# Twenty-nine half tiles masked on GpSimd in two passes, and the written order made anew

## The chip, the cores and the metric

The kernel runs on one core of a Trainium2 chip. The metric is the device time of one execution, in microseconds (us). A core has five engines with a queue each: TensorE (PE, matrix products, with its weight loads shown as PEld), VectorE (DVE), ScalarE (ACT), GpSimd (POOL) and SyncE (SP, which here only issues DMAs). GpSimd reads and writes SBUF, the on-chip memory; the products land in PSUM, from where VectorE and ScalarE take them.

## What is computed

Attention with a threshold, for 8 batches of 8 heads, 576 positions and 64 features, followed by a feed-forward layer whose hidden value is the largest of three products:

```python
scale = 1.0 / np.sqrt(q.shape[-1])
scores = scale * np.matmul(q, k.transpose(0, 1, 3, 2))
thresh = np.max(scores, axis=-1, keepdims=True) - tau            # tau = 0.02
scores = np.where(scores >= thresh, scores, -1000000000.0)
scores = scores - np.max(scores, axis=-1, keepdims=True)
attn = np.exp(scores)
attn = attn / (np.sum(attn, axis=-1, keepdims=True) + 1e-09)
out = np.matmul(attn, v)
# heads side by side: x is 4608 x 512
h = np.maximum(np.maximum(x @ w1, x @ w2), x @ w3)               # 512 -> 768
return h @ w_out                                                  # 768 -> 512
```

## The kernel before, in words

**Tiling.** A quad is four heads of one batch; there are 16 quads, two to a batch. A quad has nine chunks, and a chunk has two half tiles of 128 rows by 576 scores. That makes 144 chunks and 288 half tiles. The letters in brackets below are those of the order string.

**One half tile.** `scores` [S] makes 576 scores for each of 128 rows in PSUM. `maximum` [m] copies them to an SBUF tile `z` on VectorE with the sign turned and takes the row maximum on the way (`nm`). What follows depends on the half tile's digit in the string `MASKED`:

- digit 0: VectorE makes the threshold `th` [s]; ScalarE passes over `z` with Prelu [e], which leaves scores above the threshold nearly flat and keeps the others far off; ScalarE passes again with Exp and sums the row [n].
- digit 1: ScalarE passes once with Exp [e]; VectorE masks by comparing with exp(-tau), multiplies, and sums the row [k].
- digits 2 and 3: as 0 and 1, but the first ScalarE pass reads the scores from PSUM.

When both halves of a chunk have their sums, VectorE takes the reciprocals `rs` [r]; GpSimd multiplies each half by its reciprocal into the bf16 tile `P` [p, once a half]; SyncE issues a transposing DMA from `P` to `ptq` [t].

**The rest of the work.** [T] turns q and k on TensorE, [a] and [c] take them out of PSUM (a: ScalarE, c: VectorE or ScalarE), [q] makes the copy `qs` of q with its halves swapped (GpSimd, now and then VectorE). [O] is attention times v for a quad's two head pairs, [w] and [x] take it out to `xt`. [F] and [B] are the two parts of a piece of the feed-forward layer, for the hidden rows (`ph`) or for the output (`po`); [h] and [v] make the running maximum of the three products (h a copy on ScalarE, v a maximum on VectorE, into `hm` and at last `hT`); [u], [f], [j] copy the output, [o], [i], [d] store it. [l] loads q, k and v, [g] loads the weights to `stage` and [z] casts them on GpSimd; [y] casts v on GpSimd.

**What sets the order.** Nothing is scheduled when the kernel is built. `_Ordered` chains every engine's instructions in the order in which Python emits them, and Python emits them by reading the string `ORDER` letter by letter in `issue`. A digit behind S, T, O, F or N names one of four double banks of PSUM. So each engine's queue is its letters of `ORDER`, first to last, and an instruction that waits holds everything behind it on its engine. A later batch's scores and an earlier batch's feed-forward pieces are interleaved in this string. The last batch is split (`SPLIT`), so that its feed-forward layer comes in two parts.

**Buffers.** `z` has 9 buffers, and from the 73rd half tile on two more are taken from the pool `stage` (`half_of_z`), which is why the profile shows some half tiles under the name `stage`. `P` has 6 buffers, `hm` 3.

Of the kernel before, what the change touches and what calls it, by code (L numbers as in the profile page):

```python
# [21 lines left out]
FLAT = 2.0 ** -100  # L22

MASKED = """
220202110002002100110000100020020312000112012010100000000010100000001100
001000111010000101100000000000110001100000011110110200100000100010000000
110001101110100100010000001001100100000100101111102300000100100000001000
001000110100100001000000000100100001011110100011011100002100001000001013
"""


# [2 lines left out]
ZBUFS = 9  # L34
MORE_Z = 72
PBUFS = 6

SPLIT = {7: ((0, 1), (2, 3, 4))}
# [3 lines left out]
ytS1erkpT2agmnT3pclesqS2aqetS0meqlrnspmS1eqsT2nmpS3tnrcS0zlemS2eprmS3npmtS0npsgS1sermpS2emyS3eptmT0eplmS1ayl  # L42
meS0kynS2tssT3snkynkercperlT3pmnpmntqremS0lasprgeT3pmeS2psstnplnS0mzecesqrmS3etqkeS2gpnmS1npsmtnS0prmleS3pmS
2npsmnS0yrsmetperS2epmO1eqtnkplemnzswT2teS3rplS1empnmS3tpnssrS1klepS0mapermtS2epmT1S3nmqtnkO2qemncpS3txrskT1
# [12 lines left out]
S1lceBqmeptrskS0pulS3muS1epmS2teF0rmplnskpeS1mtO3eklekO2esrmpesBknpwxS1kutS2urmopS3nF0myeS1mBetpsmF2hlS3rkep
BlmnF0S1prnsvT3tepBmF2apsssvS1eBtqmeS0qrS3hmtS1epsmF2lnpF0mleF3koBnBrvpeBstyvS1phsS2nmF3emS0nrS1tpmBnprS2smn
F0pveF1pBsremT3ptevBpS2chF0tnmF3ekBT1nvS2aBsmlnF0qvS1eS2rtrespmS3eBmqF1hmpT2nBcpS3ekpT2O0sasvterlmpO2ekqntwS
3xklpS1eF2ssmnF0yrBnmyS3evBptemS1plhS2ssmT3eyF0rcpeF1mBpntT3vnByS2ravpS0nmtpS3nsmS1eF2srmpektepS3slmnS0Bmeqn  # L60
mT1ktuS3urS0lcpeO2rlmpelmpeO3klpelweF1kqnsxS0rkepS2tmS3eBymemepS0kuF3quT2smeBtrF1kphoS0aBmnpS3tsN2rnvplnmpS1
erkpF0tjsF3mnBpsseBvS2ihrS1pmelS0mqeF3S2mnytBpmnoS1rF0eprsvF2ntpmBeBvqF1htskpS3esS0rmetS2pnmF3pBnmF0pesvT2te
BcF1nsBrvpntBskphT2F3erS0vlapBmnF1qvS2etpBmT0hS3rscpnF2lmS1qesS0sempBemS3yF1nvtS0nmBnT2ssrmpO3etspveF0wnS1rk
BpaS3tmhS2elqsF1mlS0qnmS3ermpBF2espsmS0npvBeS3tmeS1rvpO0ntmnsmS2yxS3empF0eskyerT1mpeS2cBtnypsmelkS3ulS2muS1e
smT0O3nsrplnpO2awetmeF3rkpxseT0S1ycntS2meF0poBrnsmpnkpF1ukBurS2shBqemF3oepvS0lS2nsmqF1emBptBnvF0hrrS2speS3mp
F1emBpntT2vepF3BssaktS0nvlBemS2hS1rsmptF0nS3mpeBmtnT2F1svnF3cetBBsrnvpS2hsrqS0meS1pmeT3F2sprmaS0npBmeF3ptsvn
S1qS0mnBtqmeS2yF1prevS0epssBmnS3qmS2htpmF0nlF1keBsmBertvO3pnvepF0serwpT2nBcpF3hktS1eBsrsmpnT0S2vtpaS1remqT3S
0nmyF2qectT1BpasmS3epvS1nS0mqnF2rmpemtpT3eS1keqS0smBercntpS1mupS3emF0ukessS1rmtpnBmopkS2uskS1eO3rukekO0yxeO3
# [36 lines left out]
def kernel(  # L105
# [273 lines left out]
    def exponents(c, r):  # L379
        z = c["z", r]  # L380
        src, sign = (c[r], -1.0) if direct(c, r) else (z, 1.0)
        if masked(c["g"], c["idx"], r):
            scalar.activation(out=z, in_=src, func=AF.Exp, bias=c["nm", r], scale=-sign)
        else:
            th = c["nm", r] if direct(c, r) else c["th", r]
            scalar.activation(out=z, in_=src, func=AF.Prelu, bias=th, scale=sign, alpha=FLAT)

    def numerators(c, r):
        z, acc = c["z", r], c["sm"][:, r:r + 1]
# [89 lines left out]
    def ffn(b, part):  # L479
# [219 lines left out]
    def flow(what, fn):  # L699
        while True:  # L700
# [7 lines left out]
    line = {k: [] for k in "menkrptahvuxwcqsjf"}  # L708
# [10 lines left out]
    def issue(what, where):  # L719
# [27 lines left out]
        elif what == "m":  # L747
            c, r = line["m"].pop(0)
            maximum(c, r)
            line["e"].append((c, r))  # L750
            if not masked(c["g"], c["idx"], r) and not direct(c, r):
                line["s"].append((c, r))
        elif what == "s":
            threshold(*line["s"].pop(0))
        elif what == "e":
            c, r = line["e"].pop(0)
            exponents(c, r)
            line["k" if masked(c["g"], c["idx"], r) else "n"].append((c, r))
        elif what in "nk":
            c, r = line[what].pop(0)  # L760
            if "sm" not in c:
                c["sm"] = small.tile([128, 2], F32, name="sm")
            else:
                c["summed"] = True
            numerators(c, r)
        elif what == "r":
            c = made[line["r"].append(0) or len(line["r"]) - 1]
# [62 lines left out]
```

## Time and profile before

| what | value |
|---|---|
| runs | 442.97 us median of 3 (442.29 to 443.37) |
| profiled execution, first to last instruction | 440.2 us |
| instructions on TensorE (products), VectorE, ScalarE, GpSimd | 5188, 1248, 834, 420 |
| TensorE clock granted, mean | 0.988 of full |
| DMA | 88.50 MB in 213959 packets, 201 GB/s |
| transposing DMAs `ptq<-P` | 144, median 4.5 us from issue to landing |

The profile belongs to one execution; its span is the time from its first to its last instruction. What lies around the span (start and end of the launch) is not shown in it. The page gives each engine's busy time; the groups of instructions give count, busy time and the mean duration of one; the chain of waits follows the last instruction back to what released it, step by step. Every instruction of the program stands under L93, since a helper there records all of them, so they are told apart by the names of the tiles that they write and read, `out<-in`.

### The profile page before, as it was taken

The numbers are of one execution on the slowest core, as the hardware profiler recorded it, in microseconds if no ns is written. First come the engines' busy times: TensorE is split into PE (matmuls) and PEld (weight loads), VectorE is DVE, ScalarE is ACT, GpSimd is POOL, SyncE is SP. The second block draws the span as 40 slices with busy tenths as digits, with TensorE's granted clock in tenths as the row PEclk, the third lists the DMA queues.
The fourth block names the chain that finished last, engine by engine and source line by source line (L and its number), as shares of the span: only waits on it lengthen the run. The fifth ranks groups of instructions, "written<-read, shape, count | busy, mean of one in ns | idle before, by whom it ended". The sixth has DMA issues, their size and how long they took to land.

```text
span 440.2 us, 14283 instructions
## 1 busy us (share of the span) xinstructions
PE 418.9 (95%) x5188; PEld 313.6 (71%) x5190; DVE 393.9 (89%) x1248; ACT 403.6 (92%) x834; POOL 317.0 (72%) x420
## 2 busy tenths in 40 slices
PE   7696789999999999999999999999999999999996
PEld 6353446787788776787678777887688777786873
DVE  4888899999999999999999999999889999998542
ACT  4999999999999999999999999999999998989521
POOL 1988999998787778867786778886585776554400
PEclk9987999999999999999999999999999999999999
DMA  6999999999999999999999999999698778583812
GB/s 190 276 239 214 270 215 260 263 252 252 220 277 224 237 165 242 291 160 232 189 242 238 202 182 273 192 199 208 135 237 153 147 109 185 102 169 72 192 50 85
DMA packets 213959, 88.50 MB, mean 201 GB/s; under 512 B 189184, under 2 KB 202240, under 8 KB 213888
## 3 DMA queue, kind: packets, MB, share of 16 engines
q1 hardware_dynamic: 213360, 86.96, 95.4%
q8 instruction: 41, 0.67, 0.6%
q10 hardware_dynamic: 528, 0.62, 0.5%
q14 instruction: 30, 0.25, 0.2%
HBM read 35.65 MB, written 9.44 MB: 102 GB/s over the span
## 4 chain that ended last, share of the span: by engine, by line
PE 78%; DVE 5%; POOL 5%; issue 4%; ACT 3%; DMA 2%; SPq 1%; DVEq 0%; POOLq 0%; ACTq 0%
PE ph L93 31%; PE sc L93 26%; PE po L93 10%; PE o L93 8%; POOL P L93 4%; PE tp L93 3%; ACT z L93 3%; DVE z L93 3%; DMA qm<-in_q_dram 2%; SPq L93 1%; DVE kt L93 1%; POOL w L93 1%; DVE stage L93 0%; DVE hm L93 0%; POOL qs L93 0%
## 5 line engine op out<-in xcount | busy, mean ns | idle before, releaser
L93 POOL TENSOR_SCALAR P<-z,rs 128x576 bf16<-128x576 f32 x250 | 202.0, 819 | 59.1 <-DVE rs L93 30.4
L93 DVE TENSOR_SCALAR_CACHE_REDUCE z<-sc 128x576 f32<-128x576 f32 x250 | 183.2, 749 | 12.2 <-PE sc L93 8.1
L93 PE MATMUL sc<-kt,qs 64*128 64x256 f32 (+2 forms) x640 | 179.8, 417 | 5.5 <-DVE z L93 3.9
L93 PE MATMUL sc<-kt,qt 64*128 64x320 f32 (+2 forms) x640 | 180.9, 429 | 3.1 <-DVE z L93 1.2
L93 PE MATMUL ph<-xt,w 64*128 64x288 bf16 (+2 forms) x2160 | 172.0, 283 | 0.2 <-DVE hm L93 0.2
L93 PEld LDWEIGHTS <-w 64*128 64x128 bf16 (+1 forms) x2160 | 128.0, 94 | 31.6 <-issue 4.0
L93 ACT ACTIVATE z<-z,th 128x576 f32<-128x576 f32 x161 | 120.5, 767 | 2.2 <-DVE th L93 1.9
L93 ACT ACTIVATE z<-z 128x576 f32<-128x576 f32 x175 | 117.6, 674 | 0.2
L93 PEld LDWEIGHTS sc<-kt,qs 64*128 64x128 f32 (+1 forms) x640 | 92.4, 179 | 22.5 <-DVE z L93 8.6
L93 PEld LDWEIGHTS sc<-kt,qt 64*128 64x128 f32 (+1 forms) x640 | 92.0, 179 | 14.7 <-DVE z L93 3.5
L93 DVE SCALAR_TENSOR_TENSOR z<-z 128x576 f32<-128x576 f32 x75 | 61.7, 827 | 1.4 <-ACT z L93 1.1
L93 POOL COPY qs<-qt 64x640 f32<-64x640 f32 (+3 forms) x66 | 45.9, 695 | 19.5 <-ACT qt L93 16.1
L93 ACT ACTIVATE z<-z,nm 128x576 f32<-128x576 f32 x72 | 53.9, 767 | 0.0
L93 PE MATMUL po<-wo,hT 64*128 64x512 bf16 (+3 forms) x454 | 53.3, 354 | 0.3
L93 DVE TENSOR_TENSOR hm<-ph,hm 128x576 bf16<-128x576 f32 (+2 forms) x54 | 37.0, 685 | 9.8 <-PE ph L93 9.6
L93 ACT ACTIVATE hm<-ph 128x576 bf16<-128x576 f32 (+2 forms) x54 | 31.9, 590 | 14.3 <-PE ph L93 13.8
L93 PEld LDWEIGHTS <-hT 64*128 64x128 bf16 (+2 forms) x456 | 28.4, 95 | 18.5 <-issue 2.6
L93 DVE TENSOR_TENSOR hT<-ph,hm 128x576 bf16<-128x576 f32 (+2 forms) x54 | 36.9, 683 | 2.8 <-PE ph L93 1.0
L93 PE MATMUL o<-ptq,vb 128*64 128x512 bf16 (+2 forms) x544 | 38.7, 282 | 0.2 <-DVE z L93 0.2
L93 POOL TENSOR_SCALAR P<-stage,rs 128x576 bf16<-128x576 f32 x38 | 29.5, 783 | 11.7 <-DVE rs L93 8.4
L93 ACT ACTIVATION_READ_ACCUMULATOR z<-z 128x1 f32 x175 | 33.6, 192 | 0.0
L93 PEld LDWEIGHTS <-vb 128*64 128x64 bf16 x544 | 22.4, 111 | 14.0 <-issue 5.6
(44 smaller groups left out, 412.2 us busy)
## 6 DMA issues: line engine op xcount, KB each, us to landing
vm<-in_v_dram SPq DMA_DIRECT2D x32, 256.0 KB, 4.6
qm<-in_q_dram SPq DMA_DIRECT2D x15, 512.0 KB, 4.7
km<-in_k_dram SPq DMA_DIRECT2D x15, 512.0 KB, 5.4
out_dram<-ob SPq DMA_DIRECT2D x14, 512.0 KB, 4.5
stage<-in_moe_w_dram SPq DMA_DIRECT2D x9, 512.0 KB, 5.6
ptq<-P SPq DMA_TRANSPOSE x144, 4.5
vr<-in_v_dram SPq DMA_DIRECT2D x16, 128.0 KB, 3.8
stage<-in_moe_w_out_dram SPq DMA_DIRECT2D x3, 512.0 KB, 5.5
```

The lines of the kernel that those rows point to most:

```text
L93: ins = fn(*a, **kw)
```

## The change

Four things change together.

First, the string `MASKED` is another one, and it has a new digit, 4, on 29 of the 288 half tiles. A half tile with a 4 gets its maximum [m] and threshold [s] on VectorE as a 0 does. Then GpSimd makes two passes: `marked` [b] adds the threshold to `z`, multiplies by 2^100 and writes the result as int8 into the high bytes of a bf16 tile `far`, which so holds a very large number where the score is under the threshold and a zero elsewhere; `moved` [C] adds `far` to `z`. ScalarE then makes one pass with Exp that also sums the row [G]. The digits' counts are:

| digit | before | after |
|---|---|---|
| 0 | 187 | 174 |
| 1 | 84 | 69 |
| 2 | 14 | 10 |
| 3 | 3 | 6 |
| 4 | 0 | 29 |

Second, `ORDER` is written anew from the first letter to the last, with the letters b, C and G in it.

Third, `hm` has two buffers in place of three, and `far` is one new tile of 128x576 bf16, set to zero by VectorE at the start.

Fourth, the tile of row sums is made by whichever sum comes first (`summed`); this moves no work.

```diff
 MASKED = """
-220202110002002100110000100020020312000112012010100000000010100000001100
...
+241202210002302100100101300030022112000110010010010001000000100100001001
...
+FARS = 1
+FAR = 2.0 ** 100
...
 ORDER = """
-lllllllllT0laqqlcT1aS2lcqqgmS0S3lemS1lmnT2lmeS3lsaS0mnqlqemT3lyerclcapsnS1lS2eqmlS3qemznmS2perS1mnpsmnpT3ske
...
+llllllllllT1lacT2qqlaS1lqqcmgS3S2lemS0lnsS3mlbT1lmeClcelmayS0lGsT1lS3mqalceqlrS1mqelqmnS0lzS2eklpS1egmnprmnp
...
+    def on_pool(c, r):
+        return by_mask[2 * number[c["g"], c["idx"]] + r] == "4"
...
     def exponents(c, r):
         z = c["z", r]
         src, sign = (c[r], -1.0) if direct(c, r) else (z, 1.0)
+        if on_pool(c, r):
+            scalar.activation(out=z, in_=z, func=AF.Exp, bias=c["nm", r], scale=-1.0, accum_out=summed(c)[:, r:r + 1])
+            return
...
+    far = [one.tile([128, S], BF16, name=f"far{x}") for x in range(FARS)]
+    for t in far:
+        vector.memset(t, 0.0)
+    fars = iter(range(1 << 20))
+
+    def marked(c, r):
+
+        c["far", r] = t = far[next(fars) % FARS]
+        pool.tensor_scalar(out=t.bitcast(mybir.dt.int8).rearrange("p (n x) -> p n x", x=2)[:, :, 1],
+                           in0=c["z", r], scalar1=c["th", r], scalar2=FAR, op0=OP.add, op1=OP.mult)
+
+    def moved(c, r):
+        pool.tensor_tensor(out=c["z", r], in0=c["z", r], in1=c["far", r], op=OP.add)
...
-                    st["hm", f] = hp_.tile([128, nr, n], BF16, name="hm", bufs=3)
+                    st["hm", f] = hp_.tile([128, nr, n], BF16, name="hm", bufs=2)
...
         elif what == "s":
-            threshold(*line["s"].pop(0))
+            c, r = line["s"].pop(0)
+            threshold(c, r)
+            if on_pool(c, r):
+                line["b"].append((c, r))
+        elif what == "G":
+            exponents(*line["G"].pop(0))
+        elif what == "b":
+            c, r = line["b"].pop(0)
+            marked(c, r)
+            line["C"].append((c, r))
+        elif what == "C":
+            c, r = line["C"].pop(0)
+            moved(c, r)
+            line["G"].append((c, r))
```

More of the change, by code (lines that the diff above doesn't have):

```diff
@@ L36 @@
 PBUFS = 6
[L38 removed]
+FARS = 1
+FAR = 2.0 ** 100
+SPLIT = {7: ((0, 1), (2, 3, 4),)}
 ORDER = """
[L41 to L44 removed]
@@ new lines @@
+S2elqsmS0lnpskteprmepmnS3pmnS1qsermtpekS3epS2srtmeykeT1T0lnpmtaspknS0qsrS3emtpempncS0tpemnzsrS3smleT2S1ptmep
+rkeptncS0empS2nrS3mqtnS1mpeS0mplerklT3petmnT2psmS1ntrsS0kepsamyerS3cpS1epmtS2nmpO0emqtnmS3znrsO1lsweplmeygT0
+kyT3elS2cgxrsalmpS1eS0lkyS3ntpsmS2eprkO1epmnpmnS0qserO3mnqwepS2smS1xpktnF3ysremBpT0ermS2qthsspknF3pmatBS1epr
+vS0eztmF2eS3mpS1nlsmBpegF0svznlBkleF2S3grhmpBtnmF0peS1sssvqnBrmT3pnS2cF1eptrvBepS3mhpT0emT2zS1nsctS3nqmF2arg
+smBpelS0vpnS1mF3nzmBeS2grsesvpF1tS0esmqBnkpS3eF2mhyBmeF1rtvpF0nkBpeBstsvnS3zS2remS1hpgmeF0lpsmS3ezBsekO2nqgm
@@ new lines @@
+tnrvS1pnS3wyeF0prmT2npBmeS1psrvaO3zesmekpT0gS1xtcS2epS3mnF0qtsmF1nqrBsmeBpkhF2pteT3vBaS0zveS1mezS3mntS2qS0sr
+nmyF1epmlnlrpsskS3tnpS2meBpmtebrmF0uspulskelT2pS3cleS1CrlmnBtesmpS3ekpS2lnmO1ouqsrstmupO3ewyGkS0xprT1nF2myS3
+nypBamtS0hqF1srnmS3peBsmpS2etF0rspvnF3mqnBlsBplervS1lphF2smetpS0S3esbmF1ntBCkeF0BnmpBestvF3nsrS2vphtBrmnyS0e
+vtS2pGsmS3peF1mlS0pesrslmF2nylBympnBlvT3phlF0srcnS1tsT2eBmS3avS1eqmS2epF0tmnT3qBsmnpF1veS2tscBebF0mhoF3ekBtn
+rS1vpS2nmCBnF0srrmF1epBveT2ptkBhpF3asvBnptrS2veS0pmGS1ptT3snmF2pesrmpteS0scpnO1smqtersnpS3wS0lebmBlCmlelT1su
@@ new lines @@
+S0pluS3maO2nmGkT1ytxS0rscS3emS2pnS1mnyO0prmeqtmeO3psrewyekpS2lF1elmqnlskS0ptnBrxmpeokqS0luS3utmpF2nS1rmpeS0s
+rsBmebF3mhptT1BsakCF2esvS0eS1pmBeN3pmtnyskGoF0jprvlS1nS3primnF2pBersslmyBqhS1tevF0pemBptS2evpF3nmT0pnS1ctqS2
+nrssmpF0etBmyBphkF1elT2vBlaS3srelvqS0tnmS2qS1empF3nsmpF0nBmtS2hskF1beS3rmBnCssmF2eBvpBrsvS0phS3sGmptF2eT1rmp
+BnO0slpcnlsvpetT3rwbS1aF2pemT3lS0qntscF1npBmeBCrvS3hS0empF2tGS1mpS3esqsmF0tnBmeBrvpO3nkesvS2yxS1nmT3yS0eyrmb
+S2lasslF1meplmnCtT0esBrcpGklqS0ulS2rumplS3nS1mlpeS0ompF2elmpntsmS3qesO1kpnrsemO0pewpnrkS1yxtS3keBrymnpmS0etp
@@ new lines @@
+F1sresmS3putBpmuF0hykBptnS1svS2eprmF3tepT0mBnpS1stavF2nmqS0eF3rqmoBesBktbhS1snvF2CS0emF3emBpnBrssvpF0ekpS2te
+S1hmpBnrmS3ptGF2ssvpS1emBbtnF0mnCS3vBeF1srrhmpT2eBcpT0eS3vlpS2atmpF1GS0smnF3tsmeBbS2snrsvqS0emBCnF1smT2hBplc
+eS0plvT3nO2lqsmGtbnskO0CerrwS1xpS2amF0peS3srpmtnF1mBpnBsvpGtS3sS2hprmeT0ptF1mnF3pcBeqtT2vBaS0rnsvpT1S2empS3e
+mS0ytnscF2eyrsmyqnlS1mlS3epmBlnqmleqlrS1kepS3lmuO0lpnsmleptO1wuekS3xskS0beS1mtnF2CmesrmeS3pBreopmykS1uS0supm
+F3eoN2rysmGbtknCF1skjBiBphrT0S2vaptS3GkpF1eF0rmBqnrmBpS2svhtF3pesmS0peBtmF1pnvS2peS0tsmnF3pBresptBvbS2hmS1ep
@@ new lines @@
+mF3nCtS0mBssmeF1qvT2nBrekF0pF3ncBprsBvhptF2GvT0yT1apBrsclnS3qvlF0eqtmS1eS2pmnBplS3smnF1lshrS2smtbeBmS0CeF3ve
+S2mpnBssGO1bvempnS3wCtS2nsmF0eT1rmBpaS3kpnF2rsmS1hptBGmS0peF3rrsvqteS1smBpeS2mnpS0smepO1tsnvpesmS2btS3xkCnS0
+mF1emqerrT2sspmnS3BcpeGmptS0yruskS2uO3nmyopemptO1erswpnT2ptxS0T3ayF1pmnlcqeS0lryeS2lmS3nlpBsmetsembF0nsklqF3
+uBlkuF2yhrsoBrpnF1vptBeBCveS3hF0pmS2nT1smBbaF3nsvpS1teS2pmF0GCBmnBtsrveS1pS2rshmpF3GS0mytepBsrsmF2npF1nsvptT
+0BecpBervS3tphS0mpnS2mbntF1sT3smCeBS0asvS2eqmF3eqS1mS0GmBnS2mnF1rvS0pBsmpS3hrsmF2ptnS1smbeF0ssBmCeBsrevO1pev
@@ new lines @@
+pntsF2weqF0kBnqT1hBcpT3nS2rvptaS1mS0epF3mGqtT2mT1qBasrcS0eqS1vnS2pmF3eqmepmT0nS1trcS2npBmnprkeptS1usmF0upmeb
+tkS3eBersmpoekCS1uS3umO2epomnkS0tGS1srkpeO3smxpermO2ptrnswpkS1xptS0emF3ynF2kBysBrmhpS1evF3ytpS0nmF2persmBpte
+BskN1pershbtS0vjpF2nmiS1CnF3smBepBsrevpS1tevS0pGmF2tS3nmS1nrsBsmpeF0bsmhO3epS2weBCtmS3nvF1nS2mnF0rmS3pGBssem
+bF2ekBCF3hvBnBpvGF0trsS2rvpeS1mpF3nBmptBhskpO2erO0vxptS1rwpS3mpF0tmeF2bBeBCvnF1khF3pBGBvS0trS2vpS1mpF3ktsmF0
+rmepS2ekpBmbtkBuCueoN3ukO1uO2oxGO0wrrF2pxF1hpF0jvF2ptvF1hF3pvF0vtF2hF3vF1viF2hF0vF1vF3hF2vF0vF3hF1vO2vO3wF1x
@@ L74 @@
+F0uF3hoF1vF0vF2hF3vF0vF1hF2vF3vF0hF1vF2vF0hF3vF2vF0hF3vF2vF1uoN3uoF2jifd
 """
@@ L386, in exponents, with summed @@
             scalar.activation(out=z, in_=src, func=AF.Prelu, bias=th, scale=sign, alpha=FLAT)
+    far = [one.tile([128, S], BF16, name=f"far{x}") for x in range(FARS)]
[8 more added lines that the diff above has]
+        pool.tensor_tensor(out=c["z", r], in0=c["z", r], in1=c["far", r], op=OP.add)
+    def summed(c):
+        if "sm" in c:
+            c["summed"] = True
+        else:
+            c["sm"] = small.tile([128, 2], F32, name="sm")
+        return c["sm"]
     def numerators(c, r):
-        z, acc = c["z", r], c["sm"][:, r:r + 1]
+        z, acc = c["z", r], summed(c)[:, r:r + 1]
         if masked(c["g"], c["idx"], r):
@@ L707 @@
                 O=products(), F=pieces(), N=iter(lambda: ninths.pop(0), None))
-    line = {k: [] for k in "menkrptahvuxwcqsjf"}
+    line = {k: [] for k in "menkrptahvuxwcqsjfbCG"}
     casts = iter([w[1] for w in wl])
@@ L749, in issue @@
             maximum(c, r)
-            line["e"].append((c, r))
+            if not on_pool(c, r):
+                line["e"].append((c, r))
             if not masked(c["g"], c["idx"], r) and not direct(c, r):
@@ L760, in issue @@
             c, r = line[what].pop(0)
[L761 to L764, printed above, removed]
             numerators(c, r)
```

36 lines of the change are left out of this document (4 added, 32 removed).

## The prediction, made before the changed kernel ran

> **What bounds the kernel now.** The page's head says that three engines are nearly full, so I read the stretches next (time, then busy time and instructions of PE, PEld, DVE, ACT, POOL, then the granted clock, the DMA share and GB/s).
>
> ```profile
> span 440.2 us, 14283 instructions
> PE 418.9 (95%) x5188; PEld 313.6 (71%) x5190; DVE 393.9 (89%) x1248; ACT 403.6 (92%) x834; POOL 317.0 (72%) x420
> ...
> 20.00:80.00 60.00, 48.58 (x466) 30.18 (x468) 52.98 (x181) 59.08 (x126) 55.43 (x72) 0.91 1.14 245
> 80.00:400.00 320.00, 319.60 (x4213) 247.63 (x4211) 307.72 (x975) 312.71 (x642) 244.79 (x321) 1.00 1.01 204
> 400.00:440.00 40.00, 36.16 (x365) 25.74 (x363) 20.50 (x52) 18.12 (x41) 6.30 (x8) 1.00 0.39 101
> ```
>
> From 20 to 80 ScalarE is full (59.1 of 60) and TensorE is not. From 80 to 400 TensorE, ScalarE (313 of 320) and VectorE (308) are all full by their busy time. From 400 on only TensorE works. TensorE's busy time is modelled, so I price its work from the chain of waits, where pieces run back to back (start, length, what, instructions):
>
> ```profile
> 80.99 0.37 PE tp L93 x8
> ...
> 125.79 2.45 PE ph L93 x40
> ...
> 158.07 1.30 PE po L93 x12
> ...
> 163.66 3.85 PE o L93 x60
> ...
> 401.57 1.40 PE sc L93 x12
> ```
>
> A half tile's scores are four matmuls (eight for the fifth chunk of a quad; 1280 matmuls are 288 half tiles), so three half tiles take 1.40 us, 0.467 each. The stretches for each tile alone (time, busy, count, clock), here for sc from 0 and from 80, then ph, po, o and tp from 80, give the counts:
>
> ```profile
> 0.00:80.00 80.00, 43.47 (x262) 0.94 1.08 241
> 80.00:400.00 320.00, 145.04 (x1008) 1.00 1.01 204
> ...
> 80.00:400.00 320.00, 147.32 (x1931) 1.00 1.01 204
> ...
> 80.00:400.00 320.00, 40.95 (x360) 1.00 1.01 204
> ...
> 80.00:400.00 320.00, 34.55 (x510) 1.00 1.01 204
> ...
> 80.00:400.00 320.00, 21.44 (x404) 1.00 1.01 204
> ```
>
> So TensorE's own work from 80 to 400 is sc 1008/1280 x 288 x 0.467 = 105.8, ph 1931 x 0.0613 = 118.3, po 360 x 0.108 = 39.0, o 510 x 0.064 = 32.7, tp 404 x 0.046 = 18.7: together 314.5 of 320 us. **Only some 5.5 us are slack there.** In the first 80 us the 262 score matmuls are 59 half tiles, 27.5 us of work, shown as 43.5 busy: that is where TensorE's time is lost, because the first batch's softmax must be through before any feed-forward piece exists, and ScalarE sets its pace. The end is fixed:
>
> ```profile
> 410.93 7.96 PE ph L93 x72
> ...
> 421.82 9.78 PE ph L93 x72
> ...
> 431.87 4.41 PE po L93 x28
> ```
>
> From 411 on it is the split batch's feed-forward on TensorE, some 29 us that the change leaves as they are.
>
> **The change, part by part.** The prices of the passes are start-to-start times in the timeline (start, length), since an engine starts the next instruction before the last one's length is over:
>
> ```profile
> 400.94 0.76 ACT L93 ACTIVATE z<-z,th 128x576 f32<-128x576 f32 x1
> 401.61 0.67 ACT L93 ACTIVATE z<-z 128x576 f32<-128x576 f32 x1
> 402.19 0.19 ACT L93 ACTIVATION_READ_ACCUMULATOR z<-z 128x1 f32 x1
> 402.28 0.76 ACT L93 ACTIVATE z<-z,th 128x576 f32<-128x576 f32 x1
> ```
>
> A ScalarE pass takes 0.67 us without a sum (400.94 to 401.61) and with one (401.61 to 402.28).
>
> ```profile
> 58.92 0.75 DVE L93 SCALAR_TENSOR_TENSOR z<-z 128x576 f32<-128x576 f32 x1
> 59.60 0.75 DVE L93 TENSOR_SCALAR_CACHE_REDUCE z<-sc 128x576 f32<-128x576 f32 x1
> ...
> 147.16 0.15 DVE L93 TENSOR_SCALAR th<-nm 128x1 f32<-128x1 f32 x1
> 147.23 0.80 DVE L93 SCALAR_TENSOR_TENSOR z<-z 128x576 f32<-128x576 f32 x1
> ```
>
> VectorE's masking pass [k] takes 0.68, a threshold 0.07.
>
> *ScalarE.* Passes are 2 for digits 0 and 2, and 1 for 1, 3 and 4. Before: 2 x (187 + 14) + 84 + 3 = 489. After: 2 x (174 + 10) + 69 + 6 + 29 = 472. That is 17 passes less, 11.4 us. The digit 4's pass has both a bias tile and a sum, which no row shows together; were it the 0.76 of a whole activation, 29 x 0.09 = 2.6 us would go back.
>
> *VectorE.* Masking passes fall from 87 to 75 (-8.2 us), thresholds rise from 187 to 203 (+1.1): 7 us less.
>
> *Where.* In the first 72 half tiles (two batches) the strings hold 127 ScalarE passes before and 122 after (3.4 us), and 17 masking passes before and 21 after (+2.7 us on VectorE, which has 7 us free from 20 to 80). Only one digit 4 stands there. The other 28 stand behind, with 362 passes before and 350 after (8.0 us) and 70 masking passes before and 54 after (10.9 us, less 1.3 for thresholds).
>
> *GpSimd.* Two passes are added 29 times. The nearest rows:
>
> ```profile
> L93 POOL TENSOR_SCALAR P<-z,rs 128x576 bf16<-128x576 f32 x250 | 202.0, 819 | 59.1 <-DVE rs L93 30.4
> ...
> L93 POOL CAST vb<-vm 128x1024 bf16<-128x1024 f32 x16 | 17.4, 1086 | 3.2 <-PE o L93 2.8
> ```
>
> `marked` has the form of the P pass with an int8 result at every second byte: 0.8, at worst 1.28, the mean of two P passes that were held up (the last fence of this prediction). `moved` reads two tiles: between one P pass (0.82) and two (1.64); the cast reads 1024 elements in 1.09, so 1152 should take 1.22, and I take that. A pair is then 2.0 us, within 1.6 and 2.9; 28 pairs are 56 us, and GpSimd from 80 on goes from 245 to 301 of 320. The GPSIMD Engine Reference of the Trainium skill, section 3.1, measures a two-input add of 2048 elements at 4497 ns; that is an estimate of 1.26 us for 576, and the pair would be 2.1.
>
> *The waits added.* [b] waits for a threshold, [C] follows it on its own engine, [G] waits for [C]. Behind [b] and [C] on GpSimd stand P passes, behind those the transposing DMAs on SyncE, behind [G] the next ScalarE passes. In the new order 1.6 to 8.6 us of ScalarE work stand between the threshold and [G], and GpSimd needs 2.0: [G] is covered unless GpSimd is late by some us. The queues that would carry lateness:
>
> ```profile
> SPq L93 <- POOL P L93: 124.0, 86, 5.1
> ...
> POOL P L93 <- DVE rs L93: 38.8, 31, 5.0
> ...
> PEld L93 <- issue: 12.2, 39, 0.4
> ...
> POOL P L93 <- issue: 5.8, 4, 2.0
> ...
> PE tp L93 <- DMA qm<-in_q_dram: 1.4, 4, 0.5
> ```
>
> (who waited for whom: us, times, longest). GpSimd waits 39 us for reciprocals; part of this room takes the new passes.
>
> *The order.* By the letters, the first feed-forward piece stands behind 54 scores before and 53 after, but behind 4.0 us less of ScalarE work; from there on F and S stand almost alike. The q and k loads for the third batch move from the 50th to 52nd score to the 45th and 46th, past some P passes and transposes on SyncE. TensorE waited 1.4 us in all for such a load, so this is worth at most that. Idle time that ends in "issue", where slow instruction fetches would show, is 5.8 us on GpSimd; on PEld it is 12.2 us, but it lies beside matmuls, which are full from 80 to 400. The instruction counts hardly change, so I give the fetches nothing: at best GpSimd gets its 5.8 us back, at worst it loses as much again, and it has 75 us free from 80 to 400.
>
> *hm and far.* With two `hm` buffers a copy [h] waits for the second maximum of two pieces earlier; at the closest this stands 8 letters ahead in both orders: nothing. `far` is one memset at the start, beside the first loads, under 0.5 us; its single buffer holds nothing up, as both passes that use it run on one queue.
>
> **The sum.** The first 80 us shorten by what ScalarE is relieved of, 3.4 by the passes and 4.0 by the letters; I take 3.0, for VectorE takes some over. From 80 to 400 ScalarE and VectorE lose 8 to 10 us, but TensorE has 5.5 us to give, and never all: I take half, 2.5. The end gives nothing. So 5.5 us off the span, 440.2 to 434.7. The median of the runs, 442.97, stands 2.8 above the span, which I put down to what lies around it: **437.5 us**.
>
> **The rivals.**
>
> *TensorE is the bound already, and nothing is won behind 80 us.* For it: 314.5 of 320. Against it: the start, where ScalarE is full. With only part of the start's gain the time is 440.5 to 444, I say 442.
>
> *More is won.* If the slack goes wholly (5.5) and the start gives 4, 433.5. Against it: three engines at 97% and more leave a fixed order little to be right about.
>
> *GpSimd becomes the bound, and it is slower.* It has 320 - 245 = 75 us free from 80 to 400, so it is full when a pair costs 75/28 = 2.7 us; from there on P passes, transposes and the next batch's feed-forward come late. At 2.9 the sum is 326, 6 over, and nothing is won: 449. What could bring the pair there is this:
>
> ```profile
> 173.48 1.08 DVE L93 SCALAR_TENSOR_TENSOR z<-z 128x576 f32<-128x576 f32 x1
> ...
> 172.92 1.04 POOL L93 CAST vb<-vm 128x1024 bf16<-128x1024 f32 x1
> 173.94 2.56 POOL L93 TENSOR_SCALAR P<-z,rs 128x576 bf16<-128x576 f32 x2
> ```
>
> The masking pass starts while the cast runs and takes 1.08 in place of 0.75, and the two P passes behind it take 2.56 together. Longer GpSimd passes mean longer holds, on both sides. The Trainium skill says as much: SBUF — State Buffer, "Who interferes with whom", has GpSimd's reads and a VectorE instruction with two SBUF inputs exclude each other for a whole instruction, and Perfetto Trace Analysis, "Optimizing Scalar/DVE Operations", warns that moving work between the two might not help. The trace agrees with the first (1.08 against 0.75). Against this rival stands that 12 of the 87 masking passes go.
>
> **How the numbers follow.** The forecast gets 0.46, TensorE the bound 0.22, more won 0.12, GpSimd the bound 0.20. A measurement of this kernel tells about 0.3% (1.3 us) from no change. Faster: 0.46 + 0.12 + 0.08 of the second case (below 441.6) = 0.66; same 0.14; slower 0.20. The range, 432.5 to 446.5, leaves out a twentieth below (a little over the whole slack won) and some two thirds of the GpSimd case above.
>
> **What would show it.** ScalarE's passes at 0.67 and its sum lower by some 11 us; the first feed-forward matmuls about 3 us earlier; the two new GpSimd groups at about 0.8 and 1.2 us each, GpSimd at 300 of 320 or less, SyncE's wait for P not much longer. A pair over 2.7 us, or reciprocals done long before their P passes, would make the prediction wrong on the slow side; TensorE waiting less than now in the first 80 us by more than 4 us, on the other.

## The result, and the profile after

The changed kernel is slower: 455.73 us median (452.53 to 458.14) against 443.17 (442.29 to 444.62) of the kernel before on the same chip, a ratio of 1.0293 with an interval of 1.0235 to 1.035. The forecast was 437.5, and the time stands outside its range. The profiled execution took 454.18 us, and its span from first to last instruction is 452.0. A few single runs below stand in a slower state, most of them at a lower TensorE clock; the ratios leave them out.

The head of the page after, and the same stretches as before (time, then busy time and instructions of PE, PEld, DVE, ACT, POOL, then clock, DMA share and GB/s):

```profile
span 452.0 us, 14314 instructions
...
PE 424.5 (94%) x5190; PEld 314.5 (70%) x5190; DVE 402.3 (89%) x1241; ACT 396.8 (88%) x829; POOL 378.1 (84%) x478
...
20.00:80.00 60.00, 47.07 (x428) 28.56 (x430) 55.22 (x174) 54.20 (x112) 55.93 (x72) 0.89 1.06 222
80.00:400.00 320.00, 315.10 (x4093) 239.79 (x4091) 302.09 (x946) 306.00 (x643) 290.02 (x364) 1.00 0.97 203
400.00:452.00 52.00, 47.82 (x529) 35.26 (x525) 31.58 (x78) 23.07 (x49) 20.36 (x23) 0.99 0.40 98
```

From 20 to 80 ScalarE is busy 54.2 us instead of 59.1. That isn't relief: fewer instructions got done there on it (112 against 126) and on TensorE (428 against 466). GpSimd from 80 to 400 stands at 290 of 320, close to the forecast's 301, and not full. ScalarE's busy time fell by 6.8 us over the whole run, and VectorE's, which should have fallen by 7, rose by 8.4. The groups that say why (busy, mean ns of one, then the idle time before them); first the one row of the kernel before that the prediction did not quote:

```profile
L93 DVE SCALAR_TENSOR_TENSOR z<-z 128x576 f32<-128x576 f32 x75 | 61.7, 827 | 1.4 <-ACT z L93 1.1
```

```profile
L95 DVE SCALAR_TENSOR_TENSOR z<-z 128x576 f32<-128x576 f32 x68 | 68.8, 1014 | 1.9 <-ACT z L95 1.7
...
L95 POOL TENSOR_TENSOR z<-z,far 128x576 f32<-128x576 f32 x21 | 28.5, 1357 | 1.1
...
L95 POOL TENSOR_SCALAR far<-z,th 128x576 int8<-128x576 f32 x21 | 17.7, 843 | 4.2 <-DVE th L95 2.0 <-ACT stage L95 0.5
```

A pair of the new GpSimd passes takes 0.84 + 1.36 = 2.2 us, beside the 2.0 of the forecast. The masking passes, whose form the change does not touch, went from 827 to 1014 ns. There are fewer of them (75 in place of 87, those on `stage` counted), and they take more time. (L95 stands for the helper in the changed kernel, as L93 did before.)

**Where the time goes.** I set each half tile's start of scores against the TensorE work that the order string puts ahead of it, at the prediction's prices, and subtract the same for the kernel before. The result is how many us later than before TensorE is at that place (the last row is the end of its last product; a ninth's piece [N] of half-width products is priced at half). For the changed kernel and for those of the experiments below that the argument needs (one profiled execution each):

| half tiles ahead | after | `a_nopool` | `a_t71` | `a_one_t71` | `a_one_first` | `a_loads` | `a_loads_t17` | `b_pool29` |
|---|---|---|---|---|---|---|---|---|
| 45 | 0.2 | 0.1 | 0.5 | -1.1 | -2.6 | 0.3 | 0.6 | 0.1 |
| 54 | 3.4 | 1.8 | 3.6 | -1.4 | -2.3 | 6.8 | 3.8 | 0.1 |
| 99 | 6.6 | 4.7 | 6.5 | 1.4 | 4.6 | 13.1 | 8.3 | 6.7 |
| 153 | 6.8 | 4.8 | 6.7 | 1.5 | 4.8 | 13.3 | 8.5 | 13.5 |
| 162 | 9.2 | 7.1 | 7.0 | 3.0 | 5.9 | 13.5 | 8.7 | 15.6 |
| 270 | 10.9 | 8.7 | 9.2 | 3.2 | 7.7 | 15.7 | 11.3 | 33.2 |
| end | 11.6 | 9.3 | 9.9 | 3.5 | 8.4 | 16.4 | 12.0 | 34.2 |

So the changed kernel loses at few places: some 6.5 us between the 45th and the 99th half tile, 2.4 between the 153rd and the 162nd, and little by little 2 more behind it. Over the stretch from the 99th to the 153rd next to nothing is won or lost.

**The first place.** The timeline of the changed kernel around the 54th half tile (start, length):

```profile
64.59 2.89 POOL L95 TENSOR_SCALAR P<-z,rs 128x576 bf16<-128x576 f32 x4
...
65.21 2.88 DVE L95 SCALAR_TENSOR_TENSOR z<-z 128x576 f32<-128x576 f32 x1
...
68.84 0.66 PE L95 MATMUL sc<-kt,qt 64*128 64x256 f32 x1 [2.08 <-DVE z L95]
```

Four P passes run back to back on GpSimd (64.59 to 67.48), and a masking pass that starts during the first of them ends 0.6 us after the last: 2.88 us in place of 0.75. Behind it VectorE's maxima wait, behind these TensorE's scores (2.1 us). The kernel before has such a train too, a longer one, in the same stretch:

```profile
61.27 4.23 POOL L93 TENSOR_SCALAR P<-z,rs 128x576 bf16<-128x576 f32 x5 [0.17 <-DVE th L93]
...
65.30 0.81 DVE L93 SCALAR_TENSOR_TENSOR z<-z 128x576 f32<-128x576 f32 x1
```

There the masking pass stands at the train's end and takes 0.81. Another one begins 0.13 us before the train and takes 0.75; there it is the first P pass that is held, for 1.23 us in all. Summed over all masking passes, what they last beyond 0.75 us is 6.4 us before and 19.5 after. If I divide the 19.5 by what GpSimd runs during each held pass (an estimate from the timelines), some 10 us stand beside P passes, 6 beside copies of q and casts of v, and 1.5 beside `moved`.

A second thing comes behind this wait of TensorE, and it is in the clock column. Here is the changed kernel from 69.0 to 72.4 us, then the same stretch of `a_nopool` (an experiment below), where TensorE waits the same 2.08 us at the same place (busy time and instructions of PE, PEld, DVE, ACT, POOL, then the granted clock, the DMA share and GB/s):

```profile
69.00:72.40 3.40, 3.40 (x22) 1.36 (x24) 3.40 (x14) 0.78 (x1) 2.07 (x4) 0.50 1.35 304
```

```profile
69.00:72.40 3.40, 3.40 (x40) 2.08 (x40) 3.40 (x15) 2.14 (x5) 2.06 (x4) 1.00 1.34 291
```

At a granted clock of 0.50 TensorE gets 22 products done in place of 40. That is some 1.6 of the 4.9 us that TensorE loses from the start of this wait to the 54th half tile, and nearly all that sets the two kernels apart at the 54th half tile (3.4 against 1.8). So where such a half clock follows, a wait of TensorE costs more than its own length. Whether the wait brings it on, and why it follows in one trace and not in the other, is not shown.

**The second place.** O15, half of the attention of the fourth batch's second quad, waits for its last transpose. SyncE's queue in the changed kernel, and the piece of its chain of waits (start, length):

```profile
218.46 1.30 SPq L95 DMA_DIRECT2D vr<-in_v_dram  x2
219.86 1.84 SPq L95 DMA_DIRECT2D qm<-in_q_dram  x1
221.80 1.37 SPq L95 DMA_TRANSPOSE ptq<-P  x1
```

```profile
221.80 5.03 DMA ptq<-P
226.96 1.15 PE o L95 x8
```

The P pass for this transpose was done at 218.04. Three loads stand ahead of it in the string, so it is issued at 221.80 and lands 5.03 us later (median 3.8). Of this TensorE waits 1.8 us.

### The profile page after: what moved, and what is told of

Read it like the earlier page. It is cut to its first block, busy times and chain, and to the rows that moved or that the text cites. A ratio compares the mean times of both kernels' runs of the same rounds, so it can differ in the third digit from the quotient of the medians.

```text
span 452.0 us, 14314 instructions
## 1 busy us (share of the span) xinstructions
PE 424.5 (94%) x5190; PEld 314.5 (70%) x5190; DVE 402.3 (89%) x1241; ACT 396.8 (88%) x829; POOL 378.1 (84%) x478
## 4 chain that ended last, share of the span: by engine, by line
PE 72%; POOL 10%; DVE 8%; issue 6%; DMA 2%; ACT 1%; SPq 0%; POOLq 0%; DVEq 0%
PE ph L95 29%; PE sc L95 25%; PE po L95 8%; PE o L95 7%; DVE z L95 6%; POOL P L95 5%; PE tp L95 3%; POOL qs L95 1%; DMA ptq<-P 1%; POOL far L95 1%; DMA qm<-in_q_dram 1%; POOL vb L95 1%; DVE kt L95 1%; POOL stage L95 1%; POOL vr L95 1%
## 5 line engine op out<-in xcount | busy, mean ns | idle before, releaser
L95 POOL TENSOR_SCALAR P<-z,rs 128x576 bf16<-128x576 f32 x250 | 198.9, 807 | 21.5 <-DVE rs L95 9.6
L95 DVE TENSOR_SCALAR_CACHE_REDUCE z<-sc 128x576 f32<-128x576 f32 x250 | 183.3, 749 | 13.8 <-PE sc L95 8.3
L95 PE MATMUL sc<-kt,qs 64*128 64x256 f32 (+2 forms) x640 | 180.8, 419 | 9.1 <-DVE z L95 3.3
L95 PE MATMUL sc<-kt,qt 64*128 64x320 f32 (+2 forms) x640 | 181.8, 430 | 7.2 <-DVE z L95 3.4
L95 PE MATMUL ph<-xt,w 64*128 64x288 bf16 (+2 forms) x2160 | 170.2, 283 | 1.8 <-DVE kt L95 0.8
L95 PEld LDWEIGHTS <-w 64*128 64x128 bf16 (+1 forms) x2160 | 126.0, 94 | 35.3 <-issue 5.9
L95 ACT ACTIVATE z<-z,th 128x576 f32<-128x576 f32 x151 | 113.2, 768 | 4.7 <-DVE rs L95 2.6
L95 PEld LDWEIGHTS sc<-kt,qs 64*128 64x128 f32 (+1 forms) x640 | 93.4, 179 | 25.4 <-DVE z L95 7.2
L95 PEld LDWEIGHTS sc<-kt,qt 64*128 64x128 f32 (+1 forms) x640 | 93.2, 179 | 22.6 <-DVE z L95 8.9
L95 ACT ACTIVATE z<-z 128x576 f32<-128x576 f32 x161 | 108.4, 675 | 0.2
L95 DVE SCALAR_TENSOR_TENSOR z<-z 128x576 f32<-128x576 f32 x68 | 68.8, 1014 | 1.9 <-ACT z L95 1.7
L95 ACT ACTIVATE z<-z,nm 128x576 f32<-128x576 f32 x83 | 63.0, 769 | 3.8 <-DVE z L95 3.8
L95 POOL COPY qs<-qt 64x640 f32<-64x640 f32 (+3 forms) x66 | 45.8, 694 | 10.4 <-ACT qt L95 6.6
L95 PE MATMUL po<-wo,hT 64*128 64x512 bf16 (+3 forms) x456 | 53.4, 354 | 0.2
L95 ACT ACTIVATE hm<-ph 128x576 bf16<-128x576 f32 (+2 forms) x54 | 31.9, 591 | 16.8 <-PE ph L95 16.5
L95 DVE TENSOR_TENSOR hm<-ph,hm 128x576 bf16<-128x576 f32 (+2 forms) x54 | 37.0, 685 | 10.3 <-PE ph L95 9.9
L95 PE MATMUL o<-ptq,vb 128*64 128x64 bf16 (+2 forms) x544 | 39.8, 286 | 2.1 <-DMA ptq<-P 1.8
L95 PEld LDWEIGHTS <-hT 64*128 64x128 bf16 (+2 forms) x456 | 28.2, 95 | 18.2 <-issue 2.3
L95 DVE TENSOR_TENSOR hT<-ph,hm 128x576 bf16<-128x576 f32 (+2 forms) x54 | 37.0, 686 | 3.3 <-PE ph L95 1.3
L95 PEld LDWEIGHTS <-vb 128*64 128x64 bf16 x544 | 21.6, 112 | 19.4 <-issue 10.8
L95 POOL TENSOR_SCALAR P<-stage,rs 128x576 bf16<-128x576 f32 x38 | 29.4, 779 | 2.7 <-DVE th L95 0.8
L95 ACT ACTIVATION_READ_ACCUMULATOR z<-z 128x1 f32 x161 | 31.2, 194 | 0.0
```

The costliest lines, as they stand in the source:

```text
L95: ins = fn(*a, **kw)
```

## The experiments

The theories that the expectations name: **H**, the two new GpSimd passes hold VectorE; **L**, GpSimd is simply late, holds or not; **O**, the new order does the harm, passes or no passes; **A**, ten feed-forward pieces whose two parts now follow each other directly make TensorE wait for weights; **D**, loads and transposes stand too close to their use; **T**, a transposing DMA lands late when loads stand ahead of it. **F** and **R**, on where the holds cost, are told in their expectation. Many kernels with the new order scatter by 5 to 10 us between runs, against 1 to 3 of the kernel before, so a profile says where and the medians how much. The runs stand on several chips, each beside runs of the kernel before, so the ratios compare better than the medians.

**What is it not?** `a_nopool` leaves `marked` and `moved` out, so 29 half tiles are not masked:

```diff
-            marked(c, r)
+            pass
...
-            moved(c, r)
+            pass
```

> The changed kernel with its order as it is, but both GpSimd passes of the 29 half tiles left out (the scores under the threshold are not masked there; ScalarE's one pass follows the maximum directly). Theory H (GpSimd's reads hold VectorE's two-input masking pass, and with more GpSimd passes back to back the holds grow: 1014 ns mean against 827): the masking pass falls back to 0.83 us or less, VectorE loses some 13 us of busy time, and the time is 435 to 441. Theory O (the new order itself is worse: the place of loads, transposes and banks): it stays at 449 or more. Theory L (GpSimd is simply late, holds or not): 435 to 441 as under H.

Measured: 452.78 (451.11 to 456.55), ratio 1.0251 [1.0198, 1.0305]. Without the passes that the change is about, most of the loss is still there, as O has it, and so is the length of the masking passes:

```profile
L95 DVE SCALAR_TENSOR_TENSOR z<-z 128x576 f32<-128x576 f32 x68 | 68.7, 1014 | 1.4 <-ACT z L95 1.3
```

With that H falls, and so does L. `a_writes` puts fills of about the same length in place of the two passes, so these read nothing (29 half tiles are not masked and their values are lost):

```diff
-        pool.tensor_scalar(out=t.bitcast(mybir.dt.int8).rearrange("p (n x) -> p n x", x=2)[:, :, 1],
-                           in0=c["z", r], scalar1=c["th", r], scalar2=FAR, op0=OP.add, op1=OP.mult)
+        pool.memset(t, 0.0)
+        pool.memset(t[:, 0:256], 0.0)
...
-        pool.tensor_tensor(out=c["z", r], in0=c["z", r], in1=c["far", r], op=OP.add)
+        pool.memset(c["z", r], 0.0)
+        pool.memset(c["far", r], 0.0)
+        pool.memset(c["far", r][:, 0:64], 0.0)
```

> The changed kernel with its two GpSimd passes replaced by fills of about the same length (two for the first pass, three for the second), which write the same tiles and read nothing; the mask of the 29 half tiles is left out, and the first pass does not wait for the threshold. If GpSimd's reads are what holds VectorE (H), the masking pass falls to 0.83 to 0.88 us and the time to 438 to 445 with GpSimd's busy time unchanged. If GpSimd's time is the cost (L): 451 or more.

Measured: 454.71 (451.68 to 455.03 but for one run at 493.82, clock 0.844), ratio 1.026 [1.0224, 1.0297]. The masking pass still takes 978 ns. (The time is where L has it, but L fell with `a_nopool`.) So what holds VectorE is mostly GpSimd's older work, the P passes above all, which was there before.

`a_apart` moves the ten second parts [B] one TensorE letter on:

```diff
-kyT3elS2cgxrsalmpS1eS0lkyS3ntpsmS2eprkO1epmnpmnS0qserO3mnqwepS2smS1xpktnF3ysremBpT0ermS2q
+kyT3elS2cgxrsalmpS1eS0lkyS3ntpsmS2eprkO1epmnpmnS0qserO3mnqwepS2smS1xpktnF3ysrempT0BermS2q
...
```

> The changed kernel with ten letters of its order moved: where the second part of a feed-forward piece [B] directly follows its own first part [F] on TensorE, [B] goes behind the next TensorE letter. In the order before no pair stands so; in the changed one ten do, and weight loads wait 3.7 us in ten waits for matmuls of the same piece. Theory A (these waits are TensorE time lost): the waits vanish and 2 to 4 us are won, 451.5 to 453.5. If they lie beside other waits: 455 to 456.

Measured: 458.02 (455.5 to 460.28), ratio 1.0359 [1.033, 1.0387], above both expectations. A falls: to move them wins nothing.

**The holds.** `a_oneinput` gives all 75 masking passes a form with one SBUF input. Kept places get the weight 1 in place of their exponential; the order of the passes stays, and so does the length that they have unheld:

```diff
-            vector.scalar_tensor_tensor(out=z, in0=z, scalar=thr, in1=z,
-                                        op0=OP.is_ge, op1=OP.mult, accum_out=acc)
+            vector.tensor_scalar(out=z, in0=z, scalar1=thr, scalar2=None,
+                                 op0=OP.is_ge, op1=OP.add, accum_out=acc)
```

> The changed kernel with the 75 masking passes of VectorE in a form with one SBUF input: it writes 0 or 1 and counts, so the exponentials of these half tiles are left out as weights. GpSimd's work is as in the changed kernel. Theory H: no pass is held, the masking pass takes 0.75 us, GpSimd's own passes behind it do not stretch either, and the time falls by 10 to 15 us to 440 to 446. Theory L: GpSimd has as much work as before, the time falls by less than 4, to 451 or more. Theory O: 451 or more.

Measured: 448.72 (445.81 to 453.65), ratio 1.0126 [1.0062, 1.0189], between what H and what L and O expected. `b_oneinput` does the same to the kernel before:

> The kernel before with the same one-input form in its 87 masking passes (the exponentials as weights left out there). Theory H: the holds cost VectorE 6.4 us here (87 passes, 0.07 us each over 0.75); TensorE is the bound for most of the run, so 1 to 4 us are won: 439 to 442. Theory O and L: 442 to 444, nothing is won.

Measured: 440.51 (440.02 to 441.6), ratio 0.9965 [0.9954, 0.9977]. The holds cost the old order 1.7 us (442.23 beside it), the new one about 7 us (455.73 before): the new order does the harm, and holds are a large part of how. Both sides of a hold go with it, as `b_oneinput`'s groups show (827 and 819 ns before):

```profile
L93 POOL TENSOR_SCALAR P<-z,rs 128x576 bf16<-128x576 f32 x250 | 184.0, 747 | 77.1 <-DVE rs L93 38.9
...
L93 DVE TENSOR_SCALAR_CACHE_REDUCE z<-z 128x576 f32<-128x576 f32 x75 | 55.4, 744 | 2.0 <-ACT z L93 1.8
```

The profiled execution of `a_oneinput`, the longest of its four runs, has one long wait, 6.1 us at O15 (the second half of the attention of the eighth quad) for its last transpose; at its end the clock stands at 0.50 for 6.8 us. `a_one_first` changes only the first 36 chunks (`if c["n"] < 36:` around the same edit, 21 passes):

> The changed kernel with the one-input form of the masking pass in the first 36 chunks alone (21 passes; their exponentials as weights left out); the 54 passes behind stay as they are. Theory F (the new order's loss by holds lies in the first 115 us, where GpSimd runs P passes back to back and one masking pass was held for 2.9 us): the 82nd score matmul comes some 5 us earlier than in the changed kernel, at 109 to 110 us, and the time falls by 4 to 6, to 450 or 451. Theory R (holds cost everywhere in proportion to the passes): 21 of 75 of what all of them gave (7.0 us), 2 us, 453.5 to 454.

Measured: 452.8 (447.68 to 456.7), ratio 1.0216 [1.0171, 1.0261], between F and R; the scores that F names start 3.4 us earlier than in the changed kernel, not 5. Here 2.3 to 2.6 of the 3 us that were forecast for the start appear (the table, 45 and 54) and are lost again by the 99th half tile. `a_all3` joins one-input passes, the pieces moved apart, and the transpose for O15 one letter ahead of one load:

> The changed kernel with all masking passes in the one-input form (weights left out), the ten pairs moved apart, and the last transpose of the eighth quad issued ahead of a load that stood before it. If the loss is the sum of holds (7.0), pairs (2 to 4) and this transpose (2 or more): 441 to 445. If after the holds something else of the order bounds it: 447 or more.

Measured: 447.36 (445.17 to 454.91), ratio 1.011 [1.0078, 1.0142]: something else of the order is left. Its profile has a wait of TensorE of 2.1 us, up to 125.95, for a q load.

**Loads and transposes.** That wait led me to theory D. `a_loads` moves only letters of SyncE's queue: q and k loads earlier, and the transpose for O15 ahead of its three loads:

```diff
-rkeptncS0empS2nrS3mqtnS1mpeS0mplerklT3petmnT2psmS1ntrsS0kepsamyerS3cpS1epmtS2nmpO0emqtnmS3znrsO1lsweplmeyg
+rkeptncS0empS2nrS3mqtnS1mpeS0mplerklT3petmnT2psmS1ntllrsS0kepsamyerS3cpS1epmtllS2nmpO0emqtnmS3znrsO1sweplmeyg
...
-S2lasslF1meplmnCtT0e
+S2assF1mepmnCtlllT0e
...
```

> The changed kernel, with nothing moved but letters of SyncE's queue: the q and k loads of quads 3, 4, 5 and 6 stand where their tiles come free (2 to 12 us of TensorE work earlier), and the last transpose of the quad behind O15 stands ahead of three loads. Theory D (the order puts loads and transposes too close to their use): of the lost time the wait at O15 (2.4 us) and the loss between the 81st and the 99th score (1 us) go, and the runs scatter less: 450 to 453. Theory O (masking passes held in trains of P passes, loads do not matter while these are there): 454 to 457, same scatter.

> The same moved loads, and the masking passes of the first 36 chunks with one SBUF input (21 passes; no weights, so its output differs). Theory D: with the holds gone what was lost again between the 63rd and the 99th score (7.6 us) is the loads, so TensorE keeps its 3 us to the 99th score, and the time is 442 to 446. If the loads have nothing to do with it: 450 to 454, as without the move.

> The same moved loads, and all 75 masking passes with one SBUF input (weights left out). Theory D: 437 to 441, the early gain of some 3 us under the old kernel's time with one-input passes (440.5), runs within 2 us of each other. If something else of the new order costs time: 445 to 449.

Measured: 455.8 (454.64 to 458.73), 453.92 (453.1 to 454.25) and 451.77 (451.17 to 453.05); ratios 1.033 [1.0302, 1.0357], 1.0274 [1.026, 1.0288] and 1.0233 [1.0215, 1.0251]. The second has the edit of `a_one_first` as well, the third that of `a_oneinput`. The third stands above both of its expectations, 3 us above `a_oneinput`. D falls as it was written: earlier loads win nothing, and the table shows `a_loads` 3.4 us later than the changed kernel at the 54th half tile. SyncE's queue of `a_loads` there, then its chain:

```profile
61.16 0.49 SPq L95 DMA_DIRECT2D qm<-in_q_dram  x1
61.76 0.41 SPq L95 DMA_DIRECT2D km<-in_k_dram  x1
62.70 2.12 SPq L95 DMA_TRANSPOSE ptq<-P  x1
```

```profile
62.70 6.80 DMA ptq<-P
69.55 2.18 PE o L95 x9
```

The transpose behind two loads of 512 KB takes 6.80 us to land, against a median of 3.9, and O1 (the second half of the first quad's attention) waits 3.8 us for it. The clock then stands at 0.50 from 69.0 to 75.8. In the changed kernel's trace the 144 transposes go the same way: the 87 that are issued while no load ahead of them is in flight land after 3.1 us at the median, the 16 behind one such load after 5.2, the 41 behind two or more after 5.6. The Trainium skill, DMA: Bandwidth & Descriptors, "Queues, rings and completion order", has all DMAs of one issuing engine on one ring of each DMA engine, taken in ring order. The 6.80 us agree with that. `a_loads_t17` puts the four loads behind this transpose:

> The kernel with moved loads, but the four loads for quad 4 stand behind the transpose that O1 waits for, in place of ahead of it. Theory T (a transposing DMA lands late when loads stand ahead of it): the wait of 3.8 us for it at O1 is gone and 3 of the 3.4 us that the move cost up to the 54th score come back: 451.5 to 453.5. If the loads only take bandwidth wherever they stand: 455 to 457.

Measured: 454.94 (454.25 to 456.09), ratio 1.0297 [1.0274, 1.0321]. The wait at O1 is gone and at the 54th half tile 3.0 of the 3.4 us are back, as T has it. The whole time came down by 0.9 only (on another chip; the intervals overlap), so it ends between the two expectations. Between the 81st and the 99th half tile 2.3 us are lost, where the changed kernel loses 1.0, and there GpSimd waits once, 1.7 us, for a transpose that still reads its buffer `P`; whether that is the cause is not shown. `a_t71` undoes the three loads ahead of O15's transpose and nothing else:

> The changed kernel with that one transpose ahead of three loads, nothing else. Theory T: the 2.4 us lost between the 153rd and the 162nd score go: 452.5 to 454. If later waits take its place: 455 to 457.

Measured: 452.47 (452.42 to 453.92), ratio 1.0239 [1.0215, 1.0263]. O15's wait is gone; at the 162nd half tile the table falls from 9.2 to 7.0, and the runs lie within 1.5 us of each other. By the medians it is 3.3 us less than the changed kernel, on another chip and with intervals that overlap, so the trace carries this step. T holds. Then both together, `a_one_t71`:

> All 75 masking passes with one SBUF input (weights left out), and the transpose that O15 waits for ahead of three loads; the pieces of the feed-forward layer and all other loads as in the changed kernel. If holds and late transposes are what the new order lost: 439 to 443, near the old kernel's 440.5 with the same passes. If there is a third cause: 446 to 450, as without the move (448.7).

Measured: 444.82 (443.66 to 447.19), ratio 1.0067 [1.0041, 1.0093]: 7.65 us less than `a_t71`, which ran on the same chip beside it. The groups (mean ns 745 in place of 1014):

```profile
L95 DVE TENSOR_SCALAR_CACHE_REDUCE z<-z 128x576 f32<-128x576 f32 x68 | 50.5, 745 | 1.8 <-ACT z L95 1.7
```

That lies between the two expectations, 4.3 us above the old order with the same passes. `a_one_t71_nopool` leaves the GpSimd passes out of it too:

> The kernel with one-input masking passes and the transpose for O15 ahead of three loads, with both GpSimd passes of the 29 half tiles left out as well (their scores are not masked). If the new passes are the rest against the old order (4.3 us): 440 to 442. If the order itself is: 443.5 to 446.

Measured: 446.4 (442.98 to 449.9), ratio 1.0071 [1.0043, 1.0099]. By the medians the new passes aren't this rest. The fastest runs of the two, 442.98 and 443.66, are 0.7 us apart. A part of the rest may still be theirs: in the trace of `a_one_t71` a threshold [s] near the 98th half tile waits 1.0 us for `marked`, and TensorE 0.7 us for that threshold; the trace without the passes has no such wait.

**The passes without the order.** `b_pool29` is the old order with the two passes on 29 of its digit 0 half tiles, [b] and [C] directly behind the threshold, [G] in the place of the second ScalarE pass; `hm` has its two buffers here as well. Against the kernel before, a piece of the string:

```diff
-F3nyS1pmeBsysmF0thT2rrlpeS1clF3epsmBnqT2svBaS1e
+F3nyS1pmBsysmF0thT2rrlpeS1clF3epsmBGqT2sbCvBaS1e
...
```

> The order before, with 29 of its digit-0 half tiles (from the 73rd on, four or more apart, chosen for the most ScalarE work between threshold and sum) masked by the two GpSimd passes: [b] and [C] directly behind the threshold, the first ScalarE pass left out, the second one taking the sum as in the changed kernel. Computes all of the reference. ScalarE loses 29 passes, 19 us. Theory H (GpSimd's passes hold VectorE and come late): 446 to 452. Theory O (the passes do little harm by themselves and the new order was the harm): 440 to 444, since TensorE has some 5 us to give and no more.

Measured: 476.07 (475.62 to 477.82), ratio 1.077 [1.0751, 1.079], far above both expectations. Its stretch from 80 to 400 and its waits (who waited for whom: us, times, longest), then the same wait before:

```profile
80.00:400.00 320.00, 301.37 (x3764) 223.92 (x3764) 288.25 (x882) 272.89 (x556) 284.40 (x348) 0.99 0.92 189
```

```profile
DVE z L95 <- POOL P L95: 23.7, 31, 2.6
...
POOL P L95 <- DVE rs L95: 20.5, 15, 5.0
```

```profile
DVE z L93 <- POOL P L93: 3.0, 8, 0.8
```

GpSimd is not full here (284 of 320), and yet VectorE waits 23.7 us for P passes to free a buffer `z`: two passes, some 2.3 us together, put into GpSimd's queue make the P passes behind them late. The holds grow as well:

```profile
L95 DVE SCALAR_TENSOR_TENSOR z<-z 128x576 f32<-128x576 f32 x75 | 71.0, 952 | 1.3 <-ACT z L95 1.1
```

That is 952 ns where the same passes in the same order took 827; over all masking passes 18.1 us beyond 0.75 in place of 6.4. How the 34 us divide between lateness and holds I did not test. The loss comes evenly (the last column of the table), about 1.2 us for each pair. These two passes could not simply be put into the old order.

## Why the prediction was wrong, step by step

- **TensorE's slack** ("Only some 5.5 us are slack there"): not contradicted, and not tested either. Over the 99th to the 153rd half tile none of the table's kernels with the new order moves by more than 0.2 us against the old one, and `b_oneinput`, which relieves VectorE in the old order, won 1.7 us in all. The 2.5 us that the sum took from here did not come: at the end of the trace the changed kernel is later than at the 99th half tile, not earlier.
- **ScalarE** (17 passes at 0.67, 11.4 us): its busy time fell by 6.8. By the lengths in the two traces the passes give 10.8 us less, but there are 213 read-outs of a row sum in place of 201, since each digit 4 needs one, which gives 2.6 back; the rest I did not take apart. It decided nothing, since ScalarE, at 306 of 320, waits for others.
- **GpSimd** (2.0 a pair, 301 of 320): 2.2 and 290, the size nearly right. By the medians the new passes cost the changed kernel 3 us (other chips, the intervals overlap). By the traces it is 2.3 at the end, of which 1.6 is the half clock behind the first wait. In `a_one_t71` the medians show no cost of them.
- **hm**, put at nothing: borne out. In the waits of the traces before and after no copy [h] waits for VectorE to free an `hm`.
- **VectorE** ("7 us less"): wrong, and the first step that failed. I took a masking pass at 0.68 from rows where nothing held it, though the mean of the group was 827 ns. The holds were in the text, but as a danger of the new GpSimd passes. They are a matter of what stands beside a masking pass, and the new order put masking passes among P passes: 1014 ns, VectorE 8.4 us more. The sum has no term for this. What that is worth in time is shown by `a_one_t71` against `a_t71`: 7.65 us, the half clocks behind TensorE's waits included (the mean granted clock is 0.996 against 0.984 in the two profiled executions).
- **The order** ("worth at most" 1.4 us, F and S "stand almost alike"): wrong, and the second. I compared each engine's letters and the ScalarE work ahead of them, not what runs beside what, nor what stands ahead of a transpose on SyncE. One load group ahead of one transpose cost 2.2 us in the trace (`a_t71`).
- **The early gain of 3.0 us**: there for the most part, but only once the holds are gone (-2.6 in `a_one_first`), and spent again by the 99th half tile.
- **The rival on the slow side**, GpSimd the bound at 449: the sign and the holding mechanism right, the condition wrong. It wanted a pair of 2.7 us and a full GpSimd; there were 2.2 us and 290 of 320. The Trainium skill's rule that GpSimd's reads and a VectorE instruction with two SBUF inputs exclude each other (SBUF — State Buffer, "Who interferes with whom") agrees with the 1014 ns against 745. It was the rule to follow, but for the old passes in the new order. That the time came out on this rival's side is its sign alone, not its account.

Taken as a chain of kernels, the 12.6 us come out like this: undoing the loads ahead of O15's transpose wins 2.2 us at that place of the trace (3.3 by medians), one-input masking passes then win 7.65, the new order so mended is still 4.3 above the old one with the same passes (444.8 against 440.5), and the old order's own holds are 1.7 to take off. That is 12.5 to 13.6, on several chips. What the 4.3 us are is open. Against `b_oneinput`'s trace `a_one_t71` loses 3.5 us between the 63rd and the 99th half tile and 1.8 more up to the 162nd, where O15 still waits 0.9 us; but for the threshold near the 98th I did not take them apart further. No kernel that computes the exponentials as the reference does was faster than the one before.

## What to carry to other kernels

Where two engines exclude each other, the price of an instruction depends on its neighbour in time: take its mean from the group, not its best row, and when an order is made anew, look up which instructions it puts side by side on these two engines. In a queue that issues loads and transposes alike, look at the loads ahead of every transpose that someone soon waits for; moving a load earlier can cost more than the load's own lateness. An instruction added to a fixed order costs what stands behind it in its queue: 29 pairs of some 2.3 us cost 34 us, though GpSimd was not full.

## What was not expected of the hardware

A VectorE pass with two SBUF inputs was held not by one GpSimd instruction but by all that remained of four back-to-back P passes: 2.88 us, although each P pass takes 0.74, and GpSimd lost nothing (four in 2.89). With one input the pass took 745 ns and the P passes 747. A transposing DMA issued while two or more loads ahead of it were in flight landed after 5.6 us at the median, without any after 3.1. And at the end of a TensorE wait of 2.1 us one trace shows the granted clock at 0.50 for 3.4 us, and at the end of waits of 3.8 and 6.1 us two others show it for 6.8 us; another trace with the 2.1 us wait stays at 1.00.
